# A loop of satisfied waits on TensorE ahead of a two-layer decode kernel

## The chip, the cores and the metric

The kernel runs on one core of one Trainium2 chip. The metric is the device time of one execution in microseconds. A profile of one execution gives, beside it, the span from the first to the last instruction and what each engine did in it.

## The reference

One token for each of two sequences goes through two layers. A layer is a layer norm, attention of 32 query heads over 8 cached key and value heads of 32768 positions, and a gated feed-forward network (ReGLU), each with a residual. Everything is float32.

```python
def _A_ref(x, k_cache, v_cache, wq, wo):
    q = (x @ wq)                                  # 32 heads of 128
    scores = einsum("bhqd,bhkd->bhqk", q, k) * (Dh ** -0.5)
    p = softmax(scores)
    o = einsum("bhqk,bhkd->bhqd", p, v)
    return o.reshape(B, Sq, Hq * Dh) @ wo
def _B_ref(x, W_gate, W_up, W_down):
    h = (x @ W_gate) * (x @ W_gate > 0) * (x @ W_up)
    return h @ W_down
x = x + _A_ref(_layernorm(x), k_cache, v_cache, wq, wo)
x = x + _B_ref(_layernorm(x), W_gate, W_up, W_down)   # both lines twice
```

Both layers read the same caches and the same weights. The two caches are 268 million bytes each, so that a run that reads them once a layer moves over 1100 million bytes from HBM.

## The kernel before, in words

There are 16 pairs of sequence and key head (called heads below). For each, the kernel reads 16 MB of keys and 16 MB of values. It goes through the heads forward in the first layer and backward in the second, so that what is still in SBUF at the turn is used again.

**The arena.** Nearly all of SBUF is one tile, `arena`, of 220 units of 1 KB on each partition. `load` (line 74) takes a stretch of units and issues one DMA on SP's queue (line 76); `done` marks the units free again when the matmuls that read them have been written down. The program is built in advance, so a load that takes units which an earlier one held becomes a DMA that waits on SP's queue for the last matmul that reads the earlier content. A whole load is half of a head's keys or values: 8 MB, 64 units. The query weights `wq` of the first layer are one load of the same size. Three such loads fill 192 units; small tiles live in the other 28.

**The order.** SP's queue is strictly in order. It begins with `wq`, then the two halves of the first head's keys, then the two halves of the second head's keys, then the first head's values, and so on. The input `x` and a table of constants (`cst`) come through ScalarE's queue (lines 106 and 108).

**TensorE's work.** Its stream begins with the layer norm (`centred`, line 149: the mean, which needs `x` and the constants on VectorE, line 148) and the query projection (`queries`, line 195: 64 matmuls into `qp`, with VectorE's transposes at line 204 between its two parts). Then for each head come scores (`k_tile`, line 225, 64 matmuls for a half), the softmax in pieces (lines 235 to 259), and the values (`v_tile`, line 309; a special set of rows at line 287). Four matmuls on different groups of 32 columns run side by side. All waits between engines are put in by the tile layer; where an instruction has to wait for more semaphores than it can hold, wait instructions (EVENT_SEMAPHORE in the trace) stand ahead of it on its engine's queue.

**The entry.** `kernel` builds the program: `bacc.Bacc` puts a barrier of all engines at the start (line 536 in the profile), and the tile context at line 539 holds all else.

## Time and profile before

| | |
|---|---|
| median of 2 runs | 2578.87 us (2577.41 to 2580.33) |
| span of the profiled execution | 2575.9 us |
| TensorE matmuls busy | 1306.1 us (51%) |
| VectorE busy | 149.3 us (6%) |
| DMA | 1107.02 MB, 430 GB/s over the span |

The profiled execution's own time is not listed apart from its span; the median of the runs is 3.0 us above the span. An engine's busy time counts work of its own; register, branch, wait and DMA-issuing instructions are not in it. In the rows of the timeline the first number is the start and the second the duration, in microseconds, and the bracket at the end tells how long the engine had been idle and what ended that. A name with a q behind the engine (SPq, PEldq) is the sequencer of its queue. In the groups of one line, the three numbers with slashes are the shortest, median and longest duration in nanoseconds, and the two with "to" the first and last start. In the rows of waits the numbers are microseconds in total, times, and the longest.

### The profile page before, as it was taken

To read this page: it belongs to the slowest core of one execution; us is meant where nothing else is said; L and a number is where in the kernel's file an instruction comes from. 1 tells how busy PE (TensorE), PEld (TensorE's weight loads), DVE (VectorE), ACT (ScalarE), POOL (GpSimd) and SP (SyncE) were. 2 spreads that over 40 slices of the span, in tenths; PEclk is the share of its full clock that TensorE was granted. 3 is DMA by queue.
4 is the path that set the end of the run, shared out by engine and by line. 5 is a ranking of instruction groups with operands and counts; after the bars stand their busy time and mean duration, and the time that the engine had idled before them with its cause. 6 is when DMAs were issued, how large, how long until landed. Compare 5 with 4: busy or idle time off the path is not lost.

```text
span 2575.9 us, 19565 instructions
## 1 busy us (share of the span) xinstructions
PE 1306.1 (51%) x9256; PEld 338.5 (13%) x9256; DVE 149.3 (6%) x363; ACT 41.1 (2%) x67; POOL 3.4 (0%) x13
## 2 busy tenths in 40 slices
PE   2544454455445544545675554455445544554456
PEld 0111111111011111111121111111111101111111
DVE  0000000000000000000010000000000000000001
ACT  0000000000000000000000000000000000000000
POOL 0000000000000000000000000000000000000000
PEclk9777777777767777777778677767677777777778
DMA  9999999999999999999999999999999999999999
GB/s 425 432 430 436 430 432 436 431 432 430 434 435 429 437 431 433 420 429 426 424 416 437 430 432 436 432 434 430 434 432 431 436 431 430 436 429 422 436 424 391
DMA packets 31919, 1107.02 MB, mean 430 GB/s; under 512 B 3600, under 2 KB 3984, under 8 KB 7440
## 3 DMA queue, kind: packets, MB, share of 16 engines
q1 hardware_dynamic: 31552, 1105.61, 99.7%
q8 instruction: 72, 1.18, 0.2%
q10 hardware_dynamic: 288, 0.17, 0.0%
q14 instruction: 7, 0.06, 0.0%
HBM read 1105.70 MB, written 0.07 MB: 429 GB/s over the span
## 4 chain that ended last, share of the span: by engine, by line
DMA 68%; PE 23%; another core or an unknown queue 9%; issue 0%; DVE 0%; SPq 0%; ACTq 0%; DVEq 0%
DMA arena<-k 51%; PE sc L225 16%; DMA arena<-v 13%; PE acc L309 5%; DMA cst<-consts 2%; DMA arena<-wd 1%; DMA arena<-wq 1%; PE qp L195 1%; PE po L331 1%; DMA arena<-wgu 1%; PE op L344 0%; PE sm L257 0%; PE mp L239 0%; PE dn L384 0%
## 5 line engine op out<-in xcount | busy, mean ns | idle before, releaser
L225 PE MATMUL sc<-arena,qz 128*32 128x512 f32 x4096 | 589.7, 728 | 602.4 <-DMA arena<-k 602.4
L309 PE MATMUL acc<-arena 128*16 128x512 f32 (+1 forms) x4128 | 585.6, 720 | 587.7 <-DMA arena<-v 587.7
L225 PEld LDWEIGHTS sc<-arena,qz 128*32 128x32 f32 x4096 | 144.0, 131 | 1003.1 <-issue 689.9
L309 PEld LDWEIGHTS acc<-arena 128*16 128x16 f32 x4128 | 119.4, 109 | 1003.4 <-issue 509.9
L235 DVE TENSOR_REDUCE stat<-sc 128x1 f32<-128x1024 f32 x32 | 39.2, 1225 | 648.8 <-PE sc L225 648.8
L245 ACT ACTIVATE arena<-sc,stat 128x1024 f32<-128x1024 f32 x32 | 35.7, 1114 | 2370.3 <-DVE stat L242 2319.5
L325 DVE TENSOR_SCALAR arena<-acc,stat 128x512 f32<-128x512 f32 (+1 forms) x38 | 24.8, 665 | 779.8 <-PE acc L309 779.8
L252 DVE STREAM_TRANSPOSE arena<-arena 128x512 f32<-128x512 f32 x64 | 41.5, 687 | 2.5 <-ACT arena L245 2.5
L331 PE MATMUL po<-cst,arena 128*128 128x4 f32 x256 | 34.8, 259 | 1.9 <-DVE arena L325 1.9
L331 PEld LDWEIGHTS po<-cst,arena 128*128 128x128 f32 x256 | 32.0, 195 | 26.6 <-issue 23.5
L259 DVE RECIPROCAL stat<-sm 128x1 f32<-128x1 f32 x32 | 5.3, 166 | 435.4 <-PE sm L257 435.4
L242 DVE TENSOR_REDUCE stat<-mp 128x1 f32<-128x32 f32 x32 | 6.1, 192 | 360.5 <-PE mp L239 360.5
L362 PE MATMUL gu<-arena 128*32 128x448 f32 x128 | 20.7, 747 | 10.6 <-DMA arena<-wgu 9.4
L195 PE MATMUL qp<-arena 128*32 128x512 f32 x128 | 23.2, 838 | 4.8 <-DMA arena<-wq 2.9
L149 PE MATMUL meana<-stat,ones 128*128 128x2 f32 x4 | 0.9, 298 | 44.2 <-DVE stat L148 44.2
L239 PEld LDWEIGHTS mp<-arena,cst 128*128 128x128 f32 x64 | 13.4, 261 | 52.7 <-issue 51.0
L239 PE MATMUL mp<-arena,cst 128*128 128x32 f32 x64 | 17.3, 359 | 3.4 <-DVE arena L238 1.7
L344 PE MATMUL op<-arena,oT 128*2 128x512 f32 x112 | 14.6, 592 | 3.6 <-DVE oT L334 3.6
L257 PEld LDWEIGHTS sm<-stat,cst 128*128 128x128 f32 x64 | 9.7, 191 | 28.7 <-issue 28.7
L257 PE MATMUL sm<-stat,cst 128*128 128x1 f32 x64 | 12.4, 264 | 0.0
L334 DVE COPY oT<-po 128x4 f32<-128x4 f32 x32 | 5.2, 162 | 76.4 <-PE po L331 76.4
L384 PE MATMUL dn<-arena 128*32 128x512 f32 x32 | 6.8, 937 | 4.7 <-DVE arena L373 3.6
(62 smaller groups left out, 83.7 us busy)
## 6 DMA issues: line engine op xcount, KB each, us to landing
arena<-v SPq DMA_DIRECT2D x31, 2048.0 KB
arena<-wo SPq DMA_DIRECT2D x16, 1024.0 KB
arena<-k SPq DMA_DIRECT2D x8, 2048.0 KB
arena<-wq SPq DMA_DIRECT2D x8, 1024.0 KB
arena<-wgu SPq DMA_DIRECT2D x8, 896.0 KB
arena<-wgu SPq DMA_DIRECT2D x4, 1792.0 KB
arena<-v SPq DMA_DIRECT2D x8, 512.0 KB
arena<-wd SPq DMA_DIRECT2D x4, 1024.0 KB
```

The costliest lines, as they stand in the source:

```text
L195: nc.tensor.matmul(qp[32 * c : 32 * c + 32, B, :], xT[:, kt, :], t[0][:, c * D : (c + 1) * D], start=kt == 0, stop=kt == KT - 1)
L225: nc.tensor.matmul(sc_of[n][32 * c : 32 * c + 32, B, :], qz[:, i % 2, 28 - 4 * j : 60 - 4 * j], kt[:, ch * D : (ch + 1) * D], start=j == 0 ...
L235: nc.vector.tensor_reduce(m1[:, :1], sc_of[n], AX.XY, ALU.max)
L239: nc.tensor.matmul(mp[:, :32], same, mt[0], start=True, stop=True)
L245: nc.scalar.activation(p[0], sc_of[n].rearrange("p a b -> p (a b)"), AF.Exp, bias=nm[:, 0:1], scale=1.0, accum_out=rs[:, :1])
L252: nc.vector.transpose(pT[0][:, B * D : (B + 1) * D], p[0][:, B * D : (B + 1) * D])
L257: nc.tensor.matmul(sm[:, 0:1], same, rs[:, :1], start=True, stop=True)
L309: nc.tensor.matmul(acc[32 * c : 32 * c + 16, e * w : (e + 1) * w], pT[:, B, m, 16 * J : 16 * J + 16], vt[:, at * D + e * w : at * D + (e + ...
L325: nc.vector.tensor_scalar_mul(acs[:, t:e], acc[:, t:e], linv[:, 0:1])
L331: nc.tensor.matmul(po[:, :REP], acs[0][:, t * P : (t + 1) * P], selh[:, 4 * t : 4 * t + 4], start=t == 0, stop=t == 3)
L344: nc.tensor.matmul(op[32 * u : 32 * u + NB, :], oT[:, u, :], w, start=i == 3, stop=i == NG - 1)
L362: nc.tensor.matmul(gu[32 * j : 32 * j + 32, s, :FS], xT[:, kt, :], t[0][:, j * FS : (j + 1) * FS], start=kt == 0, stop=kt == KT - 1)
```

## The change

A new function `rehearse` runs ahead of the tile context. VectorE sets a one-column tile to zero and thereby raises the semaphore `ready` to 1. Then TensorE alone runs a loop of two laps, with 2400 waits for `ready` to be at least 1 in each. The builder packs two waits into one instruction, so a lap is 1200 wait instructions, an addition to the lap counter, and a compare and branch back. The other engines have no part in the loop and go on to their own work. The tile `none` stands in SBUF ahead of the arena, which begins 32 bytes further on in each partition.

```diff
+LAPS, LAP = 2, 2400
...
+def rehearse(nc, none, ready):
+    nc.vector.memset(none[:], 0.0).then_inc(ready, 1)
+    with nc.Fori(0, LAPS, engines=(mybir.EngineType.PE,)):
+        for _ in range(LAP):
+            nc.tensor.wait_ge(ready, 1)
...
-    with tile.TileContext(nc) as tc:
-        attention_reglu_decode(tc, *args)
+    with (
+        nc.sbuf_tensor([P, 1], F32) as none,
+        nc.semaphore() as ready,
+    ):
+        rehearse(nc, none, ready)
+        with tile.TileContext(nc) as tc:
+            attention_reglu_decode(tc, *args)
```

## The prediction

> **What bounds the kernel now.** I read the page first, for the whole: who is busy, and what ended the idle time of the others.

> ```profile
> span 2575.9 us, 19565 instructions
> PE 1306.1 (51%) x9256; PEld 338.5 (13%) x9256; DVE 149.3 (6%) x363; ACT 41.1 (2%) x67; POOL 3.4 (0%) x13
> DMA  9999999999999999999999999999999999999999
> DMA packets 31919, 1107.02 MB, mean 430 GB/s; under 512 B 3600, under 2 KB 3984, under 8 KB 7440
> ```

> The DMA digits are 9 in every slice, at 430 GB/s, while TensorE is half idle. The bytes set the end: whatever stops the DMA for a microsecond makes the run a microsecond longer, and TensorE can be late as long as the DMA has loads left that it may start. So the change must be priced in DMA time at its place, the start. There I read the timeline, then the waits of SP's queue, then the groups of line 76, which issues the big loads.

> ```profile
> 0.73 0.39 SPq L76 DMA_DIRECT2D arena<-wq  x1
> 1.16 0.47 ACTq L108 DMA_DIRECT2D cst<-consts  x1
> 43.00 0.23 DVE L148 TENSOR_SCALAR stat<-cst,stat 128x2 f32<-128x2 f32 x1 [19.48 <-DMA cst<-consts]
> 43.37 0.56 PE L149 MATMUL meana<-stat,ones 128*128 128x2 f32 x2 [43.37 <-DVE stat L148]
> ...
> 51.68 3.64 PE L195 MATMUL qp<-arena 128*32 128x512 f32 x32 [0.85 <-DVE arena L204]
> 55.13 7.05 PE L225 MATMUL sc<-arena,qz 128*32 128x512 f32 x64
> 63.07 7.07 PE L225 MATMUL sc<-arena,qz 128*32 128x512 f32 x64 [0.88 <-DMA arena<-k]
> 82.36 5.99 PE L225 MATMUL sc<-arena,qz 128*32 128x512 f32 x32 [10.18 <-DMA arena<-k]
> 102.33 9.67 PE L225 MATMUL sc<-arena,qz 128*32 128x512 f32 x64 [10.10 <-DMA arena<-k]
> ```

> ```profile
> SPq L76 <- DMA arena<-wq: 21.0, 1, 21.0
> SPq L76 <- PE qp L195: 32.3, 1, 32.3
> ```

> ```profile
> L76 SPq DMA_DIRECT2D arena<-k x2: 327/328/328, 55.4 to 62.2; - x2
> ```

> Three things are to be seen. First, TensorE does nothing until 43.37 us, because the small constants land only then; that much delay is free. Second, the arena holds three 8 MB loads: wq and the two halves of the first head's keys. The fourth load (first half of the second head's keys) needs wq's place, and SP waits for it from wq's landing at about 0.7 + 0.4 + 21.0 = 22 to 23 us, then 32.3 us for the matmuls of line 195 (qp): it is issued at 55.4. Third, the DMA had work until then: the last of the three loads landed at about 62.2 (the next load is issued when half of the first keys are done, and the matmuls at 63.07 had waited for that landing). So the fourth load came some 5 us before the DMA would have run dry. It landed just before 82.3, where TensorE picks it up.

> Afterwards TensorE has room: 64 matmuls of a loaded half take 9.67 us, and halves arrive 20 us apart (82.36 to 102.33).

> **The change, part by part.**

> *What is issued.* The built program differs from the old one ahead of the kernel alone: each engine's own instructions, their waits and their order stay as they were. In front stand a memset on VectorE that sets the semaphore, and on TensorE's queue a loop of two laps. The 2400 waits of a lap are packed: one instruction with one wait, 1199 with two, and the last wait rides on the addition that counts the lap; then a compare and branch. So 1200 wait instructions a lap, 2400 in all. Each is satisfied as soon as it is looked at; what counts is how fast TensorE's sequencer gets through them.

> *Price of one.* The groups of the wait instructions in the trace, by line:

> ```profile
> L287 PEldq EVENT_SEMAPHORE  x2: 51/51/51, 1084.3 to 1084.4; - x2
> ...
> L539 SPq EVENT_SEMAPHORE  x5: 17/28/28, 2574.8 to 2575.1; - x5
> ...
> L152 DVEq EVENT_SEMAPHORE  x4: 50/50/179, 2548.7 to 2549.0; - x4
> ...
> L309 PEldq EVENT_SEMAPHORE  x1: 51/51/51, 121.7 to 121.7; - x1
> ```

> The first row is the very thing: on TensorE two such instructions in a row with two waits each. Each is recorded for 51 ns, but what I need is start to start. Asked in windows of 10 ns, the first starts in 1084.30 to 1084.31 and the second in 1084.41 to 1084.42, so 0.11 us apart; the other such pair in the trace agrees:

> ```profile
> L287 PEldq EVENT_SEMAPHORE  x1: 51/51/51, 2342.3 to 2342.3; - x1
> ...
> L287 PEldq EVENT_SEMAPHORE  x1: 51/51/51, 2342.4 to 2342.4; - x1
> ```

> (2342.26 to 2342.27, then 2342.37 to 2342.38: 0.11 again.) The neighbours are cheaper: the row of L309 is a wait instruction with one wait, which starts in 121.68 to 121.69, and its weight load follows at 121.76, some 0.075 later; SP's five start over 0.3 us, about 0.06 to 0.075 a step; VectorE's four over 0.3, about 0.1. I take 0.111 us, the nearest row by engine and by number of waits; 0.051, the recorded duration, is a floor, 0.06 and 0.075 are the lower neighbours, and nothing in the trace shows more than 0.111 without a real wait. Two laps: 2400 x 0.111 = 266.4 us.

> [...]

> *Entry and lap ends.* TensorE passes the start barrier here, and VectorE is free at the same moment:

> ```profile
> L536 DVEq EVENT_SEMAPHORE  x1: 21/21/21, 0.7 to 0.7; - x1
> L536 PEldq EVENT_SEMAPHORE  x1: 51/51/51, 0.7 to 0.7; - x1
> ```

> With a short memset the semaphore is set at about 0.9 us. The additions and branches of two laps I put at 0.4 us, four instructions at the price above. A lap is 1201 or so instructions of 64 bytes, nearly five blocks of 16 KB, and these are fetched by DMA:

> ```profile
> q8 instruction: 72, 1.18, 0.2%
> ```

> The columns are packets, MB and share. That is 16.4 KB a packet, and 0.2% of 16 x 2575.9 / 72 = 1.1 us each. While 256 instructions pass in 28 us, the next block is easily there. Only the jump back to the lap's head may find its block gone; I add 2 us for it (between 0 and some 4).

> *Sum on TensorE.* Its own work begins at 0.9 + 266.4 + 0.4 + 2.0 = 269.7 us instead of 43.4. All that it then needs has been in place for long, so the stretch from the first matmul (43.37) to the fourth load (55.4), 12.0 us, is repeated as it was: it is TensorE and VectorE in turn, and the DMA has no part in it. The fourth load is issued at 281.7.

> *Sum on the DMA.* wq, issued at 0.73 into empty queues, was there at about 23.0 (21.0 after SP began to wait), 22.3 us. The fourth load now also meets empty queues, so it lands at 304.0; it was there at 82.3. The shift is 221.7 us. Nothing gives it back: after 304 the DMA is full again, as TensorE finishes both halves of the first keys in 7.05 + 7.07 us while the fourth load is on its way, and so the fifth and sixth are queued behind it. From there the run is the old one, shifted.

> What stays behind the waiting instructions: only TensorE's own queue. SP issues three loads, then its fourth waits for qp; VectorE waits for the first matmul after its step at 43.00; ScalarE waits for the softmax. They all wait for TensorE and add nothing.

> *The new tensor.* It takes 32 bytes ahead of the arena, so every load lands 32 bytes further on. No row shows whether that matters; rows of 64 KB are written either way, and I put it at nothing, with a gain or a loss of some microseconds not excluded.

> 2575.9 + 221.7 = 2797.6 us of span. The median of the runs before is 2578.87, 3.0 us over the profiled span, so the time is **2800 us**, 8.6% more. A measurement of this kernel tells about 2% (52 us) from no change.

> **Rivals.**

> *Cheaper waits.* If the sequencer takes the next instruction while the last is still in hand, a long run costs less than a pair. The pair stands behind queued matmuls, which speaks for it; that two pairs agree to 10 ns speaks against. At 0.075 us the loop takes 180.0, the fourth load is 86.4 us earlier than above: 2714. At SP's 0.064 it is 2400 x 0.047 = 112.8 earlier: 2687.

> *The loop hides: no change.* TensorE is idle until 43.4 us and the fourth load may come some 5 us late, so the loop is free while it ends by about 48 us: 47 / 2400 = 0.020 us an instruction. SP's shortest record, 17 ns, would do; then the time is 2579, within 2%. Against it stands TensorE's own 51 ns, which alone makes 122 us.

> *The fetch binds.* If blocks are fetched only when they are asked for, ten of them stop TensorE. A small transfer waits behind the loads' packets: the constants, issued at 1.16, needed until 43. By the packet time of 1.1 us and as much again for the way, eight blocks on the idle DMA cost 16 us, and two under load some 4 us each (between 2 and the 42 that the constants took, which are many packets): 25 us more, 2825.
> [...]

> *Half of it runs.* If the loop were left after one lap, 133.2 + 0.2 + 2.0 us go: 2665. The built branch goes back while the counter, already raised, is under 2, so two laps.

> **How the numbers follow.** The forecast, waits at 0.105 to 0.117 us and no more than 4 us at the jump, 2786 to 2817: 0.70. Cheaper waits: 0.16, of which a fifth lies under 2705. The fetch, or anything else that is dearer: 0.08. Hidden: 0.03. One lap: 0.03. The range of 2705 to 2826 takes in the forecast, most of the cheaper waits and the fetch's price; left out are the lower waits, the hidden loop, one lap and what is dearer than 2826, about 0.14 together. Of the cases only the hidden loop is within 2%: 0.03, and I leave 0.01 for faster, from a place of the arena that suits the DMA better; the rest, 0.96, is slower.

> **What would show it.** The first matmul of line 149 at about 270 us; the wait instructions of the loop some 0.111 us apart; DMA digits of 9 up to about 62 us, then near 0 until about 282, then 9 to the end; SP's wait for qp at about 259 us instead of 32.3; the fourth load landing near 304; busy times of all engines as before. It is wrong if the steps of the loop differ from 0.111, if the DMA runs in the gap, or if the rest, counted from the fourth load, is longer or shorter than before by more than a few microseconds.

## The result and the profile after

The changed kernel takes 2790.36 us (median, 2789.91 to 2790.82), against 2578.87 before: 1.0824 times as long, with a 95% interval of 1.0807 to 1.0842. The forecast was 2800. The profiled execution spans 2788.1 us, 212.2 more than before.

The page of the changed kernel, in the lines that answer to those shown before:

```profile
span 2788.1 us, 21971 instructions
PE 1306.6 (47%) x9256; PEld 336.8 (12%) x9256; DVE 149.3 (5%) x364; ACT 41.1 (1%) x67; POOL 3.4 (0%) x13
DMA  8000999999999999999999999999999999999999
GB/s 364 0 0 30 435 435 434 435 428 435 429 436 433 430 432 435 435 433 418 430 427 418 426 439 432 434 431 431 433 433 435 431 432 433 436 431 416 436 427 395
q8 instruction: 77, 1.26, 0.2%
```

Nothing became slower as such: TensorE is busy for 1306.6 us (1306.1 before), VectorE for 149.3 as before. The whole difference is the hole in the DMA line, from the end of the first slice (one slice is 69.7 us) into the fourth. The same in three stretches (columns: microseconds, busy time of TensorE, its weight loads, VectorE, ScalarE and GpSimd, the granted clock, the DMA's share and its GB/s):

```profile
0.00:62.00 62.00, 0.00 (x0) 0.00 (x0) 1.75 (x6) 1.28 (x1) 0.46 (x7) 1.00 0.96 409
62.00:282.00 220.00, 19.56 (x160) 6.02 (x164) 3.17 (x13) 0.00 (x0) 0.71 (x1) 1.00 0.05 19
282.00:2788.00 2506.00, 1287.00 (x9100) 330.76 (x9092) 144.41 (x345) 39.84 (x66) 2.27 (x5) 0.75 1.00 430
```

The DMA works for 62 us, stands for some 211 (no load moves between 62.7 and 273.6) and then runs at 430 GB/s, as before the change, to the end. The start in the timeline:

```profile
261.33 0.56 PE L150 MATMUL meana<-stat,ones 128*128 128x2 f32 x2 [261.33 <-issue]
262.15 1.93 PE L196 MATMUL qp<-arena 128*32 128x512 f32 x8 [0.26 <-DVE arena L153]
...
268.90 3.64 PE L196 MATMUL qp<-arena 128*32 128x512 f32 x32 [0.85 <-DVE arena L205]
272.36 13.92 PE L226 MATMUL sc<-arena,qz 128*32 128x512 f32 x128
...
295.96 5.72 PE L226 MATMUL sc<-arena,qz 128*32 128x512 f32 x32 [7.63 <-DMA arena<-k]
```

TensorE's first matmul stands at 261.33 instead of 43.37, and what ended its idle time is "issue": no other engine, no DMA. The 128 matmuls on the first head's keys run in one piece, since both halves have long been there. The fourth load is picked up at 295.96 instead of 82.36, 213.6 us later. SP's queue, and the loop itself by its lines:

```profile
SPq L77 <- PE qp L196: 249.7, 1, 249.7
...
L77 SPq DMA_DIRECT2D arena<-k x2: 328/328/328, 272.6 to 279.5; - x2
...
L493 PEldq EVENT_SEMAPHORE  x2400: 51/51/51, 0.9 to 260.9; - x185
...
L491 PEldq COMPARE_BRANCH  x2: 76/156/237, 131.4 to 261.1; - x2
```

SP waits 249.7 us for the query projection, 32.3 before. The loop's 2400 wait instructions start between 0.9 and 260.9 us, 260.0 / 2399 = 0.108 us apart on the mean, though each is recorded for 51 ns. Most of these steps are 0.106 us; some longer ones make the mean. Inside a lap none is over 0.28 us; from the last wait of the first lap to the first of the second it is 0.50. The jump back at 131.4 took 0.24 us (the longer of the two branches).

### The profile page after: what moved, and what is told of

It is laid out like the page before. It is cut to its first block, busy times and chain, and to the rows that moved or that the text cites. A ratio compares the mean times of both kernels' runs of the same rounds, so it can differ in the third digit from the quotient of the medians.

```text
span 2788.1 us, 21971 instructions
## 1 busy us (share of the span) xinstructions
PE 1306.6 (47%) x9256; PEld 336.8 (12%) x9256; DVE 149.3 (5%) x364; ACT 41.1 (1%) x67; POOL 3.4 (0%) x13
## 2 busy tenths in 40 slices
DMA packets 31924, 1107.10 MB, mean 397 GB/s; under 512 B 3600, under 2 KB 3984, under 8 KB 7440
## 4 chain that ended last, share of the span: by engine, by line
DMA 63%; PE 21%; another core or an unknown queue 8%; issue 8%; DVE 0%; SPq 0%; ACTq 0%; DVEq 0%
DMA arena<-k 46%; PE sc L226 14%; DMA arena<-v 13%; PE acc L310 4%; DMA cst<-consts 2%; DMA arena<-wgu 1%; DMA arena<-wd 1%; DMA arena<-wq 1%; PE po L332 1%; PE qp L196 0%; PE op L345 0%; PE sm L258 0%; PE mp L240 0%; PE gu L363 0%
## 5 line engine op out<-in xcount | busy, mean ns | idle before, releaser
L150 PE MATMUL meana<-stat,ones 128*128 128x2 f32 x4 | 0.9, 297 | 262.1 <-issue 261.3
L150 PEld LDWEIGHTS meana<-stat,ones 128*128 128x128 f32 x4 | 0.8, 248 | 262.3 <-issue 261.3
```

## The experiments

The theory: the time paid is the DMA's idle time. TensorE's own work may begin as late as 49.1 us (261.3 less the shift of 212.2) at no cost, and each microsecond beyond that costs one. The 49.1 is taken from the changed kernel alone; the other runs test it. The rivals: the arena's new place, a cost that is paid once and not by the wait, a fetch at each jump, and that the waits and not the instructions set the price. Times and ratios are against runs of the kernel before on the same chip; spans are against the 2575.9 us of its profiled execution.

### The small tensor and the moved arena, without the loop

```diff
-    with nc.Fori(0, LAPS, engines=(mybir.EngineType.PE,)):
-        for _ in range(LAP):
-            nc.tensor.wait_ge(ready, 1)
```

> The loop is left out; the small tensor, its memset and the 32 bytes by which the arena moves stay. Theory (the cost is TensorE's late start alone): no change, 2579 us within 0.3%. Rival (the arena's new place costs or gains DMA time): the time moves, by 5 us or more; the DMA's GB/s in full slices differ from 430.

Measured: 2577.23 us against 2577.22, ratio 1.0002 (0.9992 to 1.0011). The DMA runs at a mean of 430 GB/s, as before. The 32 bytes cost nothing that can be measured; all of the change's time is the loop's.

### A loop short enough to hide

```diff
-LAPS, LAP = 2, 2400
+LAPS, LAP = 2, 400
```

> Two laps of 400 waits, 200 instructions each. Theory (TensorE's loop is free until its own work would begin later than about 49 us, which is 261.3 less the shift of 212.2 in the changed kernel): the loop ends at 0.9 + 400 x 0.108 + 0.4 = 44.5 us, so 2579 us within 0.3%. Rival (every wait is paid for): 2579 + 43 = 2622 us.

Measured: 2577.46 us, ratio 0.9999 (0.9989 to 1.0009). From its groups and timeline:

```profile
L493 PEldq EVENT_SEMAPHORE  x400: 51/51/51, 0.9 to 44.6; - x134
...
44.03 0.23 DVE L149 TENSOR_SCALAR stat<-cst,stat 128x2 f32<-128x2 f32 x1 [20.68 <-DMA cst<-consts]
45.07 0.56 PE L150 MATMUL meana<-stat,ones 128*128 128x2 f32 x2 [45.07 <-DVE arena L151]
...
L77 SPq DMA_DIRECT2D arena<-k x4: 328/328/328, 57.2 to 131.5; - x4
```

The loop runs for 44 us, TensorE starts 1.7 us later than before, and the fourth load is issued at 57.2 instead of 55.4. The 1.7 us are not the loop's alone: in this run the constants were there 1.0 us later (VectorE's step at 44.03 instead of 43.00). The run is not longer. So 400 wait instructions are free, and a start of TensorE that is 1.7 us later is too: the lead of the fourth load covers it.

### A loop that comes out of the cover

```diff
-LAPS, LAP = 2, 2400
+LAPS, LAP = 2, 720
```

> Two laps of 720 waits, 360 instructions each. Theory: the loop ends at 0.9 + 720 x 0.108 + 0.4 = 79 us, 30 over the 49 that are free: 2609 us, the fourth load issued at about 90 us. Rival (every wait is paid for): 2579 + 78 = 2657 us. Rival (TensorE, half idle, makes up for a delay of this size): 2579 us.

Measured: 2608.95 us, ratio 1.0125 (1.0108 to 1.0142), span 2606.8. The page and the timeline of this kernel:

```profile
DMA  9699999999999999999999999999999999999999
```

```profile
79.57 0.56 PE L150 MATMUL meana<-stat,ones 128*128 128x2 f32 x2 [79.57 <-issue]
...
114.56 5.81 PE L226 MATMUL sc<-arena,qz 128*32 128x512 f32 x32 [7.74 <-DMA arena<-k]
```

TensorE begins at 79.57, 30.5 over 49.1, and the span is 30.9 longer than before. The dip to 6 in the second slice holds most of the loss. TensorE, busy for half of the time, makes up for none of it, because it has nothing to hurry: the bytes come later.

### One lap

```diff
-LAPS, LAP = 2, 2400
+LAPS, LAP = 1, 2400
```

> One lap of 2400 waits, no jump back. Theory: TensorE's work begins at 131.4 us as the second lap does in the changed kernel, 82 over the 49 that are free: 2661 us. Rival (a part of the 211 us is paid once, not by the lap): the time lies above 2670 us.

Measured: 2661.72 us, 1.0327 (1.0306 to 1.0348). TensorE's first matmul stands at 131.61, 82.5 over 49.1; the span of 2659.5 is 83.6 longer. No part of the cost that these runs can tell is paid once. Beside it, its instruction packets:

```profile
q8 instruction: 77, 1.26, 0.2%
```

That is as many as with two laps: the second lap of the changed kernel fetched nothing. Its trace says the same: the packets of TensorE's queue (q8) start at 26.7, 53.9, 79.3 and 106.6 us, in the first lap, and the next at 262.6, after the loop.

### Twelve short laps, and two long ones

The first has the same 2400 instructions in twelve laps, the second twice as many in two.

```diff
-LAPS, LAP = 2, 2400
+LAPS, LAP = 12, 400
```

> Twelve laps of 400 waits: the same 2400 wait instructions, twelve laps' ends instead of two. Theory (the jump back costs what the trace of the changed kernel shows, 0.3 us and no fetch, as the loop's instructions stay on the core): 10 more lap ends of 0.4 us, less the steps saved while blocks are fetched: 2790 to 2796 us. Rival (a jump back brings its block anew, 2 us or more each): 2810 us or more, with more instruction packets than 77.

```diff
-LAPS, LAP = 2, 2400
+LAPS, LAP = 2, 4800
```

> Two laps of 4800 waits, 2400 instructions or 9.4 blocks of 16 KB a lap. Theory of the price: 4800 x 0.108 = 518, TensorE's work begins at 520 us: 2579 + 520 - 49 = 3050 us. [...]

Measured: 2794.96 us (1.0844, 1.0813 to 1.0875) and 3057.62 us (1.1863, 1.1829 to 1.1898). The groups of the loop's lines and the instruction packets, first of the kernel with twelve laps, then of that with two long ones:

```profile
L493 PEldq EVENT_SEMAPHORE  x2400: 51/51/51, 0.9 to 264.1; - x185
L491 PEldq COMPARE_BRANCH  x12: 76/208/240, 22.7 to 264.3; - x12
...
q8 instruction: 73, 1.20, 0.2%
```

```profile
L493 PEldq EVENT_SEMAPHORE  x4800: 51/51/51, 0.9 to 526.3; - x192
L491 PEldq COMPARE_BRANCH  x2: 76/1921/3766, 261.8 to 526.5; - x2
...
q8 instruction: 93, 1.52, 0.2%
```

Twelve laps of 200 instructions need one packet more than the kernel before; a jump back takes 0.2 us. Ten more lap ends lengthen the loop by 3.2 us (264.1 against 260.9). The time is 4.6 us longer; the 1.4 us between lie within the spread of the runs (the two of the kernel before lie 2.9 apart). The rival of a fetch at each jump falls. A lap of 2400 instructions does not stay: the jump back stands for 3.77 us, and 21 packets come on top of the 72, somewhat more than the 18.7 that two laps would need at the rate of the kernel before (72 packets for 18512 matmuls and weight loads of TensorE, 257 for each packet). Nine of them start before the jump, eleven between it and the end of the loop, so that both laps were fetched. The time is 7.6 us over the 3050 expected: 3.8 of them are the jump, and most of the rest are steps of 0.1087 us on the mean instead of 0.108. So a second lap of 1200 instructions of TensorE came without a packet, and one of 2400 with eleven; where between the two the limit lies was not tried.

### One wait in each instruction

The number of instructions stays at 2400, and each holds one wait instead of two. The no-operation keeps two waits from being packed and is merged with its wait: the trace has 2400 wait instructions, under the line of the no-operation (L494), and none under that of the wait.

```diff
-        for _ in range(LAP):
+        for _ in range(LAP // 2):
             nc.tensor.wait_ge(ready, 1)
+            nc.tensor.nop(nofuse=True)
```

> The same 2400 instructions on TensorE, with one wait in each instead of two (a no-operation between two waits keeps them from being packed, and is itself merged away). Theory A (each wait is looked at by itself, so the step goes by waits): half of 0.106, 0.053 us a step; TensorE's work begins at 129 us: 2579 + 129 - 49 = 2659 us. Theory B (the instruction is what costs): 0.106 a step as before, 2790 us. Theory C (a fixed part and a part for each wait, as the pair of a one-wait instruction and a weight load before the change suggests): 0.075 a step, begin at 181, 2711 us.

Measured: 2791.15 us, 1.0828 (1.0796 to 1.0859), with TensorE's first matmul at the same place as in the changed kernel:

```profile
L494 PEldq EVENT_SEMAPHORE  x2400: 51/51/51, 0.9 to 260.9; - x185
...
261.33 0.56 PE L150 MATMUL meana<-stat,ones 128*128 128x2 f32 x2 [261.33 <-issue]
```

Half the waits at the same time: the instruction is what costs, and a second satisfied wait in it is free on TensorE. Theories A and C fall.

### The loop on other queues

The same loop ahead of ScalarE's two small loads, and then ahead of SP's big ones. The first:

```diff
-    with nc.Fori(0, LAPS, engines=(mybir.EngineType.PE,)):
+    with nc.Fori(0, LAPS, engines=(mybir.EngineType.Activation,)):
         for _ in range(LAP):
-            nc.tensor.wait_ge(ready, 1)
+            nc.scalar.wait_ge(ready, 1)
```

> The same loop on ScalarE's queue, ahead of the two small loads that this queue issues. By SP's step of 0.062 us it takes 149 us. Theory (what counts is when TensorE can begin): x and the constants land at about 153 us on idle DMA queues, TensorE begins then, 104 over the 49 that are free: 2683 us. Rival (only a wait on TensorE's own queue costs): 2579 us.

Measured: 2725.75 us, 1.0575 (1.0545 to 1.0606); both expectations missed. Its groups and its timeline:

```profile
L493 ACTq EVENT_SEMAPHORE  x2400: 17/38/38, 0.9 to 192.4; - x185
...
192.58 0.39 ACTq L107 DMA_DIRECT2D x<-x  x1
193.00 0.45 ACTq L109 DMA_DIRECT2D cst<-consts  x1
...
195.18 0.23 DVE L149 TENSOR_SCALAR stat<-cst,stat 128x2 f32<-128x2 f32 x1 [0.45 <-DMA cst<-consts]
195.55 0.56 PE L150 MATMUL meana<-stat,ones 128*128 128x2 f32 x2 [195.55 <-DVE stat L149]
```

The price was wrong, taken over from SP: ScalarE's step is 191.5 / 2399 = 0.080 us on the mean, the jump back included, not 0.062. With the loop's measured end the theory gives the time: TensorE begins at 195.55, 146.5 over 49.1, and the span of 2724.2 is 148.3 longer than before. It needs no wait on TensorE's own queue; whatever delays its first matmul is paid alike. The rival falls.

The second:

```diff
-    with nc.Fori(0, LAPS, engines=(mybir.EngineType.PE,)):
+    with nc.Fori(0, LAPS, engines=(mybir.EngineType.SP,)):
         for _ in range(LAP):
-            nc.tensor.wait_ge(ready, 1)
+            nc.sync.wait_ge(ready, 1)
```

> The same loop on SP's queue, ahead of all big loads. By the step of 0.062 us it takes 149 us. Theory (the DMA's idle time is what is paid, and a loop ahead of the first load has no load in flight to hide behind): 2579 + 149 = 2728 us. Rival (some 49 us are free here too): 2680 us.

Measured: 2731.24 us, 1.0597 (1.0566 to 1.0628), 153.9 more than the 2577.37 beside it.

```profile
L493 SPq EVENT_SEMAPHORE  x2400: 17/28/28, 0.9 to 155.1; - x185
...
3.86 0.56 PE L150 MATMUL meana<-stat,ones 128*128 128x2 f32 x2 [3.86 <-DVE stat L149]
...
155.32 0.39 SPq L77 DMA_DIRECT2D arena<-wq  x1
```

The first load is issued at 155.32 instead of 0.73, 154.6 later, and all but 0.7 of that is paid. SP's loop is the cheapest for an instruction (0.064 us) and, ahead of the first load, has no cover at all: it costs more than the longer one on ScalarE. TensorE's first matmul stands at 3.86 us here, 39.5 earlier than before, since the constants find no big load under way; so it is the DMA's idle time that is paid, and not TensorE's late start as such.

On these two queues the lap did not stay. The instruction packets, of 8 KB here, of the loop on ScalarE and then of that on SP (7 before the change):

```profile
q14 instruction: 27, 0.22, 0.0%
...
q14 instruction: 28, 0.23, 0.0%
```

Of those on this queue during the loop nine start before the jump and eleven behind it, in both kernels. The first instruction of the second lap starts 2.4 us (ScalarE) and 2.6 us (SP) after the branch does, 0.30 on TensorE. That the second lap needs no fetch is shown for TensorE alone.

## Why the prediction was right

The mechanism held at every step but the fetch at the jump, and the time came out within 10 us of the forecast, inside the forecast's own 2786 to 2817. It is not owed to errors that cancel: the loop was 6.4 us cheaper, the jump's 2 us were not paid, and nothing of that size went the other way. By its terms:

| term | predicted | measured |
|---|---|---|
| a wait instruction, start to start | 0.111 us | 0.108 |
| the loop, 2400 of them | 266.4 us | 260.0 (0.9 to 260.9, the end of the first lap in it) |
| lap ends, the jump's fetch included | 0.4 + 2.0 us | 0.3 to 0.4 for each of two, no fetch |
| TensorE's first matmul | 269.7 us | 261.3 |
| from there to the fourth load | 12.0 us | 11.3 (272.6) |
| until TensorE picks it up | 22.3 us | 23.4 (295.96) |
| shift of the span | 221.7 us | 212.2 |

- *What bounds the kernel.* That it is the DMA, and that TensorE's lateness is free up to about 48 us, is shown by the short loop (free), the middle one (30.5 us over, 30.9 paid) and the loop on SP (no cover). The start of TensorE less the shift of the span gives 47.3 to 49.1 us in the seven runs with a loop on TensorE or ScalarE that comes out of the cover; the prediction's sum had 269.7 - 221.7 = 48.0. Its "some 5 us" of lead for the fourth load do not follow from the rows beside them (62.2 - 55.4 = 6.8), but the runs give 4 to 6 (47.3 to 49.1 less 43.4). The traces show the idle DMA itself: the longest stretch in which no load moves is 29.1 us in the middle run, 144.0 with the loop on ScalarE, 210.9 in the changed kernel and 476.4 with two long laps, where the spans grew by 30.9, 148.3, 212.2 and 478.8. The one to four microseconds between were not traced to a cause.
- *The price of one.* The step that was mis-sized. The two pairs in the trace before gave 0.111; in a long run it is 0.108 on the mean, 6.4 us less over the loop. The rival of cheaper waits (0.075 or less) falls by the same row. The row was chosen for its engine and its number of waits. The engine was the right criterion (ScalarE 0.080, SP 0.064); the number of waits was not, as the kernel with one wait in each shows. The pair of a one-wait instruction and a weight load, 0.075 apart, which fed the rival of cheaper waits, measured something else: how soon a weight load follows a wait.
- *The jump.* 2 us were put down for a fetch that did not come, since the lap's instructions had stayed: the changed kernel shows 77 instruction packets with two laps, as with one. The rival of the fetch falls too: the first lap's blocks came by DMA (packets at 26.7 to 106.6 us), and yet no instruction of the loop starts more than 0.30 us after the one ahead of it, which is at the jump. No run shows the 2 us on TensorE: the branch back took 0.24 us with laps of 1200 instructions and 3.77 with 2400. Nearest to it are ScalarE and SP, where the lap was fetched again and its first instruction started 2.4 and 2.6 us after the branch.
- *Half of it runs, and the loop hides.* Both are excluded by the 2400 instructions in the trace and by the hole in the DMA line.
- *Nothing gives it back.* The lag is 213.6 us where the fourth load is picked up and 212.2 at the end. The 1.4 us between lie within the spread of the runs (the two of the kernel before lie 2.9 apart).
- *The new tensor.* Put at nothing; measured, 1.0002 (0.9992 to 1.0011).

## What to carry to other kernels

In this case a delay on TensorE, which is not the bottleneck, cost what it took out of the DMA's time (30.5 us beyond the cover, 30.9 paid). So look for the first transfer that needs this engine to have worked, and for when the transfers ahead of it run dry. Here that made some 48 us free and every microsecond after them dear, though TensorE idles for half of the run. A satisfied wait instruction was not free: TensorE took 0.108 us for each, ScalarE 0.080 and SP 0.064. Price it by its start-to-start time on that very engine, not by its recorded duration and not by another engine's.
